# Polysketch attention followed by an RWKV channel mix: four half-batch stages replaced by a batch-wise pipeline with a list-scheduled issue order

## The chip, the cores and the metric

The kernel runs on one core of one Trainium2 chip. The metric is the device time of one execution in microseconds (us). The profile of one execution gives a "span", from its first to its last instruction; the time of the same execution lies about 2 us above it (130.03 and 128.0 us for the changed kernel). PE is the matmul engine, PEld its weight loads, DVE the vector engine, ACT the scalar engine, POOL the GpSimd engine, SP the engine that issues most DMAs.

Each execution is marked fast or slow; slow means over 1.5% above the fastest run of the same kernel. A ratio is the mean time of one kernel's fast runs over the mean of the other's fast runs in the same rounds, so it is not quite the ratio of the medians that stand beside it.

## The reference

The inputs are q, k and v of 4 batches, 4 heads, 1088 tokens and 32 columns, all f32. Each head's q and k are turned into 64 features: `S1` and `S2` (8 x 32 each) give two vectors of 8, and the features are their outer product. The attention is linear, so that a sum over all tokens of a batch is needed before any token of that batch can be finished. The output of the attention then goes through a token shift, two matmuls with a squared ReLU between them, and a sigmoid gate.

```python
def phi(x):
    a = einsum('rd,bhsd->bhsr', S1, x)
    b = einsum('rd,bhsd->bhsr', S2, x)
    return einsum('bhsi,bhsj->bhsij', a, b).reshape(..., 64)
q_p, k_p = phi(q), phi(k)
kv = einsum('bhsf,bhsd->bhfd', k_p, v)          # needs every token of the batch
z = sum(k_p, axis=2)
x = (q_p @ kv) / (q_p . z + 1e-6)               # (4, 1088, 128) after merging heads
# ... the RWKV channel mix
xk = mu_k * x + (1 - mu_k) * x_prev             # x_prev: the token before, 0 at the start
xr = mu_r * x + (1 - mu_r) * x_prev
out = sigmoid(xr @ w_r) * (relu(xk @ w_k)**2 @ w_v)    # w_k 128 x 1024, w_v 1024 x 128
```

## The kernel before

It works on halves (two batches each), with 64 tokens of each of two batches on the 128 partitions. It makes the features of K of half 0, then of half 1 mixed with those of Q of half 0, and only then starts the channel mix ("MoE" below) in one loop over groups of 512 rows. Matmuls for the sums of K look like this; the sum z comes from a matmul of its own:

```python
for h in range(H):
    for b2 in range(2):                       # the two batches of this half
        rows = slice(64 * b2, 64 * b2 + 64)
        nc.tensor.matmul(kv[hp:hp + 64, b2, ...], kp[rows, t - t0, h]..., tok["v%d" % half][rows, h, t, :], ...)
for b2 in range(2):
    nc.tensor.matmul(kv[:64, b2, 64:64 + HR], ab[rows, t - t0]..., ab[rows, t - t0, :, 1, :], ...)
# ... cut: the transposes of K and q, partly on DVE (transp_hd), partly as PE matmuls with the identity (transp_tok)
```

The last stage is a fixed loop that mixes the MoE of one group with the Q features of groups further on:

```python
for n in range(nn + 3):
    g, cp = divmod(n, 4)
    if n < nn: mm1(g, cp)                     # h = w_k^T XK, then relu on ACT
    if cp == 0 and g + 3 < NQ: q1(g + 3)      # features of q, group g+3
    if cp == 1 and g + 2 < NQ: q5(g + 2)      # x = qp . kv, token shift
    # ... cut: q2, Q4, rr, sq
    if 2 <= n < nn + 2: mm2(*divmod(n - 2, 4))   # o += k^2 w_v
    if n >= 6 and cp == 2: fin(g - 1)
```

## Time and profile before

Three runs: 143.38, 139.47 and 143.05 us (median 143.05).

| | kernel before |
|---|---|
| profile span | 136.2 us |
| first MoE matmul (L347) | 64.1 us |
| busy share PE / DVE / ACT | 73% / 57% / 51% |
| share of the longest chain: PE / DVE / ACT / DMA / issue | 50% / 18% / 13% / 8% / 8% |

These are lines of the page of the kernel before: its span, the busy time of each engine (share of the span, and number of records), the clock row (tenths of full rate in 40 slices), the queue that carries instructions (packets, MB, share of 16 DMA engines), and the shares of the chain that ended last.

```profile
span 136.2 us, 4574 instructions
PE 98.8 (73%) x2054; PEld 75.1 (55%) x2065; DVE 78.3 (57%) x155; ACT 69.2 (51%) x117; POOL 8.4 (6%) x29
PEclk9999999986999999999999999986999999999998
q8 instruction: 16, 0.26, 0.8%
PE 50%; DVE 18%; ACT 13%; DMA 8%; issue 8%; SPq 1%; DVEq 0%; ACTq 0%
```

No engine is near full, and the chain goes through all of them. The word "issue" is time in which an engine waited for nothing that the profile shows: 8% of the span.

The same chain in order of time (start in us, length in us, what):

```profile
18.91 1.92 issue
23.33 1.71 PE tp L154 x32
26.04 2.59 issue
37.66 0.87 PE tp L154 x32
64.08 0.39 PE h L347
```

The same 32 K transposes take 1.71 us at 23 us and 0.87 us at 37.7 us, so PE ran at half rate in the first part, although the clock row shows 9 there. The MoE starts at 64 us.

The table by stretches of the kernel before shows which engine works when. Its columns are the stretch, its length, busy us and records of PE, PEld, DVE, ACT and POOL, the granted clock, the DMA share and GB/s.

```profile
0.00:30.00 30.00, 15.59 (x413) 13.55 (x417) 10.19 (x26) 3.56 (x7) 8.45 (x29) 0.99 0.94 244
30.00:60.00 30.00, 25.64 (x928) 21.97 (x924) 13.32 (x24) 11.39 (x28) 0.00 (x0) 0.95 0.02 4
60.00:90.00 30.00, 21.48 (x297) 14.48 (x298) 22.67 (x46) 22.05 (x37) 0.00 (x0) 1.00 0.03 11
```

DVE and ACT, which carry the MoE's squares and ReLUs, do little in the first 60 us. This is the room that the change goes for. The inputs arrive in the first 30 us (DMA share 0.94).

### The profile page before, as it was taken

To read this page: it belongs to the slowest core of one execution; us is meant where nothing else is said; L and a number is where in the kernel's file an instruction comes from. 1 tells how busy PE (TensorE), PEld (TensorE's weight loads), DVE (VectorE), ACT (ScalarE), POOL (GpSimd) and SP (SyncE) were. 2 spreads that over 40 slices of the span, in tenths; PEclk is the share of its full clock that TensorE was granted. 3 is DMA by queue.
4 is the path that set the end of the run, shared out by engine and by line. 5 is a ranking of instruction groups with operands and counts; after the bars stand their busy time and mean duration, and the time that the engine had idled before them with its cause. 6 is when DMAs were issued, how large, how long until landed. Compare 5 with 4: busy or idle time off the path is not lost.

```text
span 136.2 us, 4574 instructions
## 1 busy us (share of the span) xinstructions
PE 98.8 (73%) x2054; PEld 75.1 (55%) x2065; DVE 78.3 (57%) x155; ACT 69.2 (51%) x117; POOL 8.4 (6%) x29
## 2 busy tenths in 40 slices
PE   3250958659997789496929949549949689698970
PEld 2140948458896658374626646346645466465650
DVE  3685030300158572285799595595396795977761
ACT  4010011101461423626886777674687767989950
POOL 7802004000000000000000000000000000000000
PEclk9999999986999999999999999986999999999998
DMA  3999999930000000000000002002002011021013
GB/s 103 335 275 305 301 248 224 302 58 5 5 5 0 5 5 5 7 0 5 0 2 5 0 0 82 0 0 77 0 0 82 0 40 42 0 77 76 5 77 115
DMA packets 5010, 9.79 MB, mean 72 GB/s; under 512 B 1520, under 2 KB 1904, under 8 KB 4992
## 3 DMA queue, kind: packets, MB, share of 16 engines
q1 hardware_dynamic: 3120, 6.69, 16.0%
q0 software_dynamic: 1856, 2.82, 8.9%
q8 instruction: 16, 0.26, 0.8%
q14 instruction: 2, 0.02, 0.0%
q10 hardware_dynamic: 16, 0.00, 0.0%
HBM read 7.80 MB, written 2.23 MB: 74 GB/s over the span
## 4 chain that ended last, share of the span: by engine, by line
PE 50%; DVE 18%; ACT 13%; DMA 8%; issue 8%; SPq 1%; DVEq 0%; ACTq 0%
PE kv L188 9%; DMA tok_v_66<-in_v_dram 8%; PE tp L154 8%; PE qtp L277 7%; PE o L367 7%; PE h L347 6%; DVE qp L270 5%; DVE XK L333 4%; PE abwp L250 4%; PE abp L166 4%; PE kv L195 3%; PE xps L317 2%; ACT PP_150 L332 2%; ACT PP_149 L332 2%; DVE den L262 1%
## 5 line engine op out<-in xcount | busy, mean ns | idle before, releaser
L174 DVE TENSOR_TENSOR kp<-ab 128x1024 f32<-128x1024 f32 (+1 forms) x10 | 10.6, 1064 | 23.3 <-ACT ab L170 23.1
L277 PE MATMUL qtp<-ident,qp 128*128 128x128 f32 x68 | 9.7, 284 | 13.9 <-DVE qp L270 11.8
L347 PE MATMUL h<-XK,wk 128*128 128x512 bf16 (+1 forms) x61 | 18.7, 374 | 0.5
L170 ACT COPY ab<-abp 128x256 f32<-128x256 f32 (+1 forms) x10 | 3.4, 341 | 26.6 <-PE abp L166 26.4
L277 PEld LDWEIGHTS qtp<-ident,qp 128*128 128x128 f32 x68 | 7.4, 142 | 16.9 <-ACT r L381 13.1
L188 PE MATMUL kv<-tok_v_66,kp 64*64 64x32 f32 x272 | 9.6, 269 | 8.1 <-issue 4.5
L188 PEld LDWEIGHTS kv<-tok_v_66,kp 64*64 64x64 f32 x272 | 8.9, 185 | 9.7 <-issue 9.7
L195 PE MATMUL kv<-ab 64*64 64x32 f32 x136 | 11.3, 243 | 0.0
L270 DVE TENSOR_TENSOR qp<-an,abw 128x1024 f32<-128x1024 f32 (+1 forms) x9 | 10.5, 1165 | 0.3
L317 PE MATMUL xps<-qpT,kvbd 128*64 128x256 f32 (+3 forms) x80 | 9.4, 359 | 0.0
L195 PEld LDWEIGHTS kv<-ab 64*64 64x64 f32 x136 | 8.6, 163 | 0.0
L283 ACT COPY qpT<-qtp 128x512 f32<-128x512 f32 (+1 forms) x9 | 5.1, 566 | 4.8 <-PE qtp L277 4.8
L166 PE MATMUL abp<-SW,kT_131 128*32 128x64 f32 x136 | 5.0, 314 | 3.5 <-DVE kT_131 L147 3.5
L285 DVE COPY qpT<-qtp 128x512 f32<-128x512 f32 (+1 forms) x9 | 5.9, 651 | 2.5 <-PE qtp L277 2.5
L188 PE MATMUL kv<-tok_v_67,kp 64*64 64x32 f32 x272 | 6.5, 222 | 0.8 <-issue 0.8
L333 DVE SCALAR_TENSOR_TENSOR XK<-xps,mu_k,PP_150 128x512 bf16<-128x512 f32 (+1 forms) x5 | 3.2, 644 | 6.5 <-ACT PP_150 L332 6.5
L188 PEld LDWEIGHTS kv<-tok_v_67,kp 64*64 64x64 f32 x272 | 5.9, 133 | 1.8 <-issue 1.5
L317 PEld LDWEIGHTS xps<-qpT,kvbd 128*64 128x64 f32 x80 | 4.5, 136 | 4.1 <-issue 1.7
L154 PE MATMUL tp<-ident,tok_k_68 128*32 128x128 f32 x136 | 6.5, 345 | 0.2 <-ACT qpT L283 0.2
L156 ACT COPY kT_132<-tp 128x512 f32<-128x512 f32 (+1 forms) x5 | 2.6, 523 | 7.9 <-PE tp L154 7.9
L347 PEld LDWEIGHTS <-wk 128*128 128x128 bf16 x72 | 5.7, 99 | 0.9 <-issue 0.7
L386 DVE TENSOR_TENSOR osb<-o,r 128x512 f32<-128x512 f32 (+1 forms) x9 | 5.9, 655 | 0.5 <-PE o L367 0.5
(235 smaller groups left out, 215.4 us busy)
## 6 DMA issues: line engine op xcount, KB each, us to landing
out_dram<-osb SPq DMA_DIRECT2D x7, 256.0 KB, 2.0
hd_k_70<-in_k_dram SPq DMA_DIRECT2D x1, 544.0 KB, 4.0
tok_v_66<-in_v_dram POOLq DMA_DIRECT2D x1, 544.0 KB, 8.4
hd_k_71<-in_k_dram SPq DMA_DIRECT2D x1, 544.0 KB, 5.7
tok_v_66<-in_v_dram SPq DMA_DIRECT2D x1, 544.0 KB, 11.5
tok_k_68<-in_k_dram POOLq DMA_DIRECT2D x1, 544.0 KB, 10.4
tok_k_68<-in_k_dram SPq DMA_DIRECT2D x1, 544.0 KB, 15.9
tok_q_69<-in_q_dram POOLq DMA_DIRECT2D x1, 544.0 KB, 12.5
```

Source lines behind the costliest of these rows:

```text
L154: nc.tensor.matmul(tp[D * h:D * h + D, t * P:t * P + P], tok[x][:, h, t0 + t, :], ident[:], skip_group_check=True, tile_position=(0, D * h))
L166: nc.tensor.matmul(abp[32 * c:32 * c + 32, t * 64:t * 64 + 64], kT[half][:, t0 + t, 32 * c:32 * c + 32], SW[:, 0, :, :2, :], skip_group_ch ...
L174: nc.vector.tensor_mul(kp[:, :n], _ap(a_, list(a_.ap[1:]) + [[0, R]]), _ap(b_, list(b_.ap[1:3]) + [[0, R]] + [b_.ap[3]]))
L188: nc.tensor.matmul(kv[hp:hp + 64, b2, (h // 2) * D:(h // 2) * D + D], kp[rows, t - t0, h].rearrange("p i j -> p (i j)"), tok["v%d" % half] ...
L195: nc.tensor.matmul(kv[:64, b2, 64:64 + HR], ab[rows, t - t0].rearrange("p h x r -> p (h x r)"), ab[rows, t - t0, :, 1, :], start=False, st ...
L270: nc.vector.tensor_mul(qp[g][:, :n], _ap(a_, list(a_.ap[1:]) + [[0, R]]), _ap(b_, list(b_.ap[1:3]) + [[0, R]] + [b_.ap[3]]))
L277: nc.tensor.transpose(p[:, t * P:t * P + P], qp[g][:, t, 2 * pair:2 * pair + 2].rearrange("p h i j -> p (h i j)"), ident[:])
L285: nc.vector.tensor_copy(o, p[:, :n * P])
L317: nc.tensor.matmul(o[64 * pair:64 * pair + 64], kvbd[:, 2 * half + b2, pair, :], qpT[g][:].rearrange("p r t (b s) -> p r t b s", b=2)[:, p ...
L333: nc.vector.scalar_tensor_tensor(XK[:, half * NT + T:half * NT + T + m, :].rearrange("p t s -> p (t s)"), src, mu_k[:], PP[half][:, T:T + ...
L347: nc.tensor.matmul(h[:, c, :n * P], wk[:, (2 * cp + c) * P:(2 * cp + c + 1) * P], XK[:, 4 * g:4 * g + n, :].rearrange("p t s -> p (t s)"))
L367: nc.tensor.matmul(ops[g][:, t * P:t * P + P], k2[:, c, t * P:t * P + P], wv[:, 2 * cp + c, :], start=(cp == 0 and c == 0 and t == 0), sto ...
```

## The change

The intent is to start the MoE after one batch instead of after all the features, and to keep every engine supplied from then on.

- The stages run batch by batch. A batch's 1088 tokens lie in 9 slots of 128.
- q is loaded by head and slot and transposed in 32 x 32 blocks on DVE; K is transposed on PE.
- The sums kv and z come from one accumulation: the moving operand is v's 32 columns followed by 32 ones. The K sums are 288 matmuls with 32 columns of weights each.
- Each piece of work becomes a task with an engine, a duration, what it depends on and which buffer it takes. A list scheduler in the build sets the order in which instructions are issued.
- Zero matmuls are put where the plan shows PE idle before 20 us, to keep its clock up (33 in all: 9 at the start, 24 in gaps).
- All PSUM copies of the transposed q features go to ACT; before, half of them were on DVE.

```diff
+NWARM = 9
+KARR = [5.3, 14.2, 21.3, 24.8]           # when the plan expects k of each batch
+T0F, FILL, COLD = 5.3, 20.0, 8.0
+# ... VARR, QARR, WARR, T0, TAU, HOP cut
-                    nc.tensor.matmul(kv[hp:hp + 64, b2, ...], kp[rows, t - t0, h]..., tok["v%d" % half][rows, h, t, :], ...)
-                nc.tensor.matmul(kv[:64, b2, 64:64 + HR], ab[rows, t - t0]..., ab[rows, t - t0, :, 1, :], ...)
+                for x in range(2):
+                    hp = 64 * (h % 2) + 32 * x
+                    nc.tensor.matmul(kv[hp:hp + 32, (h // 2) * 64:(h // 2) * 64 + 64],
+                                     y[:, t, h, 4 * x:4 * x + 4]..., _ap(vh, [[off, 2], [1, D]]), ...)   # v, then ones
+    T["KT" + n] = Task("PE", .35, lambda ...: kt_pe(b, i), [KARR[b]], [("aux", ["KTA" + n])], mode=2)
+    T["AB" + n] = Task("PE", .17, ...)
+    T["KV" + n] = Task("PE", .36, ...)
+    # ... some 380 further tasks cut
+    order, start, end = list_order(T, slots, HOP, WINDOW, SWITCH, COLD)
+    busy = T0F
+    for n in order:
+        if T[n].eng == "PE":
+            if busy < start[n] < FILL:
+                fill(int((start[n] - busy) / (0.43 if busy < COLD else 0.22)))     # zero matmuls
+            busy = end[n]
+        T[n].emit()
```

## The prediction

> **What bounds the kernel now.** No engine does. In the busy table PE has 73% of the span, DVE 57%, ACT 51%; the chain of waits runs through all (PE 50%, DVE 18%, ACT 13%, DMA 8%). Until the first MoE matmul (L347, 64.1 us in the chain in order of time) the features of K and Q are made: DVE works 10.2 us of the first 30 and 13.3 of the next 30, ACT 3.6 and 11.4 (table by stretches). The kv sums wait for v until 13.6 us. From 64 us the MoE takes 9 to 10 us per group of 512 rows, in one serial loop: XK, den, qp on DVE, qtp on PE, o and h matmuls, relu on ACT, PP, XK again. DVE and ACT are then busy about 74%.
>
> The page's clock row shows 9 at the start, but durations contradict it: 32 K transposes (L154) take 1.71 us at 23 to 32 us and 0.87 at 37.7. PE ran at half rate until about 34 us. [...]
>
> **What the change does.** MoE can start after batch 0 alone. With start-to-start times of the trace (ACT: relu of 1024 columns 0.92 us, 512 columns 0.47; DVE: qp of 1024 1.14, square 0.61, XK of 512 0.67) I sum the new kernel:
> - ACT about 70 us: relu 31.5, sigmoid 4, copies of kT, ab, abw, qpT 20, PP and XB 11.5, rest 3. Old sum about 58.
> - DVE about 73 us: kp 10.5, qp 10.5, q transposes 6, den chains 8.5, XK 7.5, squares 21, outputs 5, rest 4. Old sum about 66.
> - PE about 65 us warm; kv and z take 288 matmuls where 680 ran (27.4 us busy before); zero matmuls only fill gaps.
>
> So the change adds elementwise work; it removes waiting, and half-clock PE in the first 34 us.
>
> **Fill.** k of batch 0 lands near 5 us (before, the first k load landed 4.0 us after issue). Chain: kT, ab, three kp (2.6), kv, z, q1, den 1.2, qp, qtp, qpT, xps, PP, XK: about 15 us with hand-overs, so the first MoE matmul is at about 20 us instead of 64. By then ACT and DVE have done 12 to 14 us of work; some 57 us remain on each. If the in-order queues, two shared PSUM buffers and one o buffer let them run at 85%, that takes 67 us; the tail (squares, o matmuls, output product, four DMAs issued in turn) adds 4. Span about 92 us. The times lie 3 to 7 us above the profile's 136.2, so I predict **97 us, range 89 to 108**. Faster by over 2%: 0.97; within 2%: 0.01; slower: 0.02.
>
> **What would show it.** First L512 matmul at 18 to 24 us; 12 K transposes in about 0.35 us from about 8 us on; from 20 us to the tail DVE and ACT at least 80% occupied by start-to-start time; no wait for input DMA over 2 us after the first; no long wait of PE on fin for the single o buffer.
>
> **What would make it wrong.** Arrivals later than the order written into the kernel assumes: the order is fixed, so one late tensor stalls everything behind it, and the counted zero matmuls leave a gap in which the clock drops. [...] The two shared PSUM buffers (about 85 uses, each PE to ACT and back) may hold occupancy to 70%: span 105. Occupancy near 95% would give a span near 84.

Its sum is 20 + 67 + 4, put at about 92 us of span, and 5 us more for the time.

## The result and the profile after

The changed kernel took 130.03, 129.87 and 130.20 us in its fast runs (135.08 in a slow one). The ratio to the kernel before is 0.938, with a 95% interval of 0.927 to 0.950. It is faster, as predicted, but by 6% and not by the predicted 32%: 130 us lies well outside the range of 89 to 108.

The same lines of the page of the changed kernel:

```profile
span 128.0 us, 4696 instructions
PE 103.3 (81%) x2061; PEld 70.5 (55%) x2075; DVE 74.4 (58%) x148; ACT 77.3 (60%) x156; POOL 11.2 (9%) x44
PEclk9999999999769999999999999999999999999996
q8 instruction: 16, 0.26, 0.9%
PE 59%; ACT 13%; DVE 10%; issue 8%; DMA 4%; ACTq 1%; another core or an unknown queue 0%; DVEq 0%
```

DVE and ACT do about what I had summed (74.4 and 77.3 us against 73 and 70). PE is busy 103.3 us, where I had 65. The chain now runs through PE for 59% of the span.

The chain of the changed kernel in order of time, up to the first MoE matmul:

```profile
1.51 5.45 DMA S<-in_S_dram
12.32 1.31 PE ktp L284 x24
16.86 1.17 issue
22.82 2.21 issue
26.25 0.79 PE ktp L284 x24
30.50 3.00 issue
39.83 0.38 PE h L512
```

The MoE starts at 39.8 us, not at 20. Three stops called "issue" take 6.4 us of that (1.17 + 2.21 + 3.00). The first work waits for the small matrix S until 7.0 us. PE is at half rate until about 13 us (24 records of K transposes: 1.31 us at 12.32 us, later 0.79), although the clock row shows 9 there as well.

The list of waits of the changed kernel (engine, what waited, for what: us in total, times, longest) names the instructions that stood at those stops:

```profile
DVE S8r L229 <- DMA S<-in_S_dram: 3.2, 1, 3.2
PE qtp L408 <- issue: 3.0, 1, 3.0
PE abwp L377 <- issue: 2.2, 1, 2.2
PE kv L321 <- issue: 1.2, 1, 1.2
```

They have nothing in common: a transpose, a feature matmul, a sum. What they share is their place in PE's instruction stream. Counted from 0, with weight loads, matmuls and the few waits of PE's sequencer together, the last records before the three stops are 448, 704 and 960, that is 256 apart. In the kernel before, the stops at 18.91 and 26.04 us stand at 448 and 704 too, and two short ones at 42.3 and 46.1 us (0.87 and 0.84 us) at 1728 and 1984, also multiples of 256 further on.

The table by stretches of the changed kernel, with the two stretches after the first MoE matmul cut at the batch periods (a batch is 8 ReLUs of 1024 columns in two groups of 512 rows):

```profile
0.00:20.00 20.00, 15.53 (x311) 10.07 (x311) 6.11 (x18) 4.32 (x11) 11.16 (x44) 1.00 1.00 220
20.00:40.20 20.20, 14.16 (x253) 8.51 (x243) 9.62 (x27) 7.45 (x21) 0.00 (x0) 0.92 0.67 146
40.50:63.90 23.40, 21.19 (x500) 15.37 (x502) 18.38 (x34) 17.97 (x37) 0.00 (x0) 1.00 0.09 21
63.90:86.30 22.40, 21.23 (x500) 15.36 (x502) 15.75 (x27) 18.09 (x37) 0.00 (x0) 1.00 0.09 20
```

In the steady part PE is busy 21.2 of 23.4 and 22.4 us (91% and 95%), ACT 77% and 81%, DVE 79% and 70%. PE's figures are a little too low, since 12 and 13 of a batch's 16 h matmuls have a record here. So the missed 36 us of span (92 expected, 128.0 measured) fall into two parts: 19.8 us before the first MoE matmul (39.8 instead of 20) and 16.2 us after it (88.2 instead of 72).

### The profile page after: what moved, and what is told of

Read it like the earlier page. It is cut to its first block, busy times and chain, and to the rows that moved or that the text cites. A ratio compares the mean times of both kernels' runs of the same rounds, so it can differ in the third digit from the quotient of the medians.

```text
span 128.0 us, 4696 instructions
## 1 busy us (share of the span) xinstructions
PE 103.3 (81%) x2061; PEld 70.5 (55%) x2075; DVE 74.4 (58%) x148; ACT 77.3 (60%) x156; POOL 11.2 (9%) x44
## 3 DMA queue, kind: packets, MB, share of 16 engines
q1 hardware_dynamic: 7762, 6.82, 23.1%
## 4 chain that ended last, share of the span: by engine, by line
PE 59%; ACT 13%; DVE 10%; issue 8%; DMA 4%; ACTq 1%; another core or an unknown queue 0%; DVEq 0%
PE o L531 9%; PE ktp L284 9%; PE h L512 7%; PE qtp L408 7%; PE kv L321 6%; ACT k L517 6%; PE xps L427 5%; PE abwp L377 5%; PE zps L222 5%; DVE XK L442 5%; DMA S<-in_S_dram 4%; PE abp L295 3%; ACT qpT L417 2%; ACT kT L288 2%; DVE k L523 2%
## 5 line engine op out<-in xcount | busy, mean ns | idle before, releaser
L517 ACT ACTIVATE k<-h 128x1024 bf16<-128x1024 f32 (+1 forms) x36 | 35.2, 994 | 4.5 <-PE h L512 2.2
L523 DVE TENSOR_TENSOR k<-k 128x1024 bf16<-128x1024 bf16 (+1 forms) x36 | 23.4, 659 | 11.8 <-ACT k L517 11.7
L531 PE MATMUL o<-wv,k 128*128 128x128 bf16 x272 | 20.9, 220 | 1.4 <-DVE k L523 1.1
L531 PEld LDWEIGHTS <-k 128*128 128x128 bf16 x272 | 16.4, 99 | 7.4 <-DVE k L523 3.4
L417 ACT COPY qpT<-qtp 128x384 f32<-128x384 f32 x24 | 10.7, 498 | 7.8 <-PE qtp L408 7.8
L307 DVE TENSOR_TENSOR kp<-ab 128x768 f32<-128x768 f32 x12 | 11.5, 955 | 4.1 <-ACT ab L300 4.1
L222 PE MATMUL zps<-zero 128*128 128x512 bf16 x33 | 11.7, 476 | 1.0 <-DVE warm L155 1.0
L321 PE MATMUL kv<-tv,kp 128*32 128x64 f32 x576 | 10.7, 221 | 1.2 <-issue 1.2
L284 PE MATMUL ktp<-ident,tk 128*32 128x128 f32 x288 | 11.5, 309 | 0.0
L402 DVE TENSOR_TENSOR qp<-an,abw 128x768 f32<-128x768 f32 x12 | 11.1, 953 | 0.1
## 6 DMA issues: line engine op xcount, KB each, us to landing
tv<-in_v_dram POOLq DMA_DIRECT2D x3, 256.0 KB, 10.8
```

The costliest lines, as they stand in the source:

```text
L222: nc.tensor.matmul(zps[:], zero[:], _ap(zero[:], [[0, 4], [1, P]]), skip_group_check=True)
L284: nc.tensor.matmul(p[D * h:D * h + D, t * P:t * P + P], tk[b][:, h, 3 * i + t, :], ident[:], skip_group_check=True, tile_position=(0, D * h))
L307: nc.vector.tensor_mul(y[:], _ap(a_, list(a_.ap[1:]) + [[0, R]]), _ap(b_, list(b_.ap[1:3]) + [[0, R]] + [b_.ap[3]]))
L321: nc.tensor.matmul(kv[hp:hp + 32, (h // 2) * 64:(h // 2) * 64 + 64], y[:, t, h, 4 * x:4 * x + 4].rearrange("p i j -> p (i j)"), _ap(vh, [[ ...
L417: nc.scalar.copy(x[:], src)
L517: nc.scalar.activation(x[:, :, :w], live.pop(("h", g, cp))[:, :, :w], RELU)
```

## The theories

**T1, fill:** PE stops at block boundaries of its instruction stream, because the fetch of the next block waits while the input loads fill the DMA engines (DMA share 1.00 before 20 us, 0.67 from 20 to 40.2). The trace shows the fetches: queue q8 moves 16 packets of 16,384 bytes. With 256 records between stops, that is 64 bytes per record, by division. In the changed kernel the first three packets start at 15.22, 22.28 and 30.87 us and take 1.32 to 1.37 us each; the three stops end at 18.03, 25.02 and 33.50 us, 1.3 to 1.5 us after a packet is done. The next packet then starts 4.3, 5.9 and 4.3 us after a stop's end, that is after PE has entered a new block (18.03 to 22.28, 25.02 to 30.87, 33.50 to 37.76); the inputs land until about 35 us. From there on this lag is 0.7 us and less (41.74 to 42.32, 46.24 to 46.84, 52.16 to 52.74), and PE does not stop at a boundary again.

**Rival to T1:** the clock and the hand-overs between engines make the fill long, and the stops only take time in which PE would have waited anyway. A third candidate is the late landing of S.

**T2, steady part:** PE is the limit, because its work is about 90 us and not 65. **Rivals to T2:** ACT is the limit; or the two shared PSUM buffers and the fixed order are (the risk that the prediction named); or the order is poor since the planner was given too short durations.

## The experiments

All runs but one gave a right result; `half_of_o` is wrong. Edits are against the changed kernel. The ratios are those on record; their verdict is "faster" for the changed kernel and "unclear" for every other one, so the argument rests on the first h, the stops and the periods more than on the times. "First h" is the start of the first MoE matmul, "periods" are the distances of the ReLUs 0, 8, 16 and 24, all from the profile.

| run | first h, us | periods, us | span, us | fast times, us | ratio to before (95%) |
|---|---|---|---|---|---|
| changed kernel | 39.8 | 23.4, 22.4, 22.1 | 128.0 | 130.03, 129.87, 130.20 | 0.938 (0.927 to 0.950) |
| changed_again | 40.0 | 23.4, 22.4, 22.1 | 128.2 | 130.25, 129.91, 129.29, 129.72 | |
| no_gap_fill | 37.5 | 23.4, 22.4, 23.6 | 127.1 | 129.18, 128.52, 127.35, 128.16 | 0.927 (0.918 to 0.937) |
| no_zero_matmul | 38.4 | 23.4, 22.4, 23.5 | 128.0 (slow) | 127.23, 125.50 | 0.913 (0.896 to 0.931) |
| late_loads | 32.1 | 26.2, 22.4, 23.6 | 124.5 | 126.65, 125.10 | |
| S_first | 41.2 | 23.4, 22.4, 22.1 | 129.4 | 131.41, 130.99, 130.74 | 0.947 (0.940 to 0.955) |
| kv_64_columns | 34.3 | 23.6, 22.6, 22.3 | 123.1 | 125.12, 123.90, 124.68 | |
| half_of_o | 43.4 | 22.6, 21.5, 22.5 | 129.9 (slow) | 128.45, 126.88 | |
| half_qpT_on_DVE | 38.8 | 24.0, 22.9, 24.4 | 130.3 | 132.29, 131.66, 133.33 | |
| twice_h | 39.5 | 25.1, 24.1, 23.4 | 133.3 | 135.37, 135.83, 136.54 | 0.978 (0.968 to 0.989) |
| fewer_wide | 34.8 | 24.1, 23.1, 22.7 | 124.9 | 126.98, 126.39, 125.55, 126.66 | 0.910 (0.902 to 0.918) |
| wide_late_S | 31.5 | 24.1, 23.1, 22.7 | 121.6 | 123.83, 125.57, 124.15 | 0.896 (0.885 to 0.908) |
| measured_durations | 39.4 | 21.7, 23.2, 23.1 | 128.1 | 130.11, 130.55, 131.59, 131.67 | 0.943 (0.933 to 0.952) |
| mixed_tiles_fill | 29.6 | 28.5, 22.6, 22.3 | 123.1 | 125.16, 125.61, 125.61, 125.69 | 0.901 (0.894 to 0.908) |
| mixed_tiles_no_fill | 30.5 | 25.2, 22.6, 22.3 | 120.7 | 122.78, 124.04 | 0.885 (0.862 to 0.908) |
| mixed_tiles_q2 | 29.4 | 24.4, 22.6, 22.3 | 118.9 | 120.89, 122.15 | 0.883 (0.871 to 0.895) |

From the ReLU 24 to the end it is 19.4 to 19.7 us in every run but `twice_h` (20.3). The third period of `no_gap_fill`, `no_zero_matmul`, `late_loads`, `half_qpT_on_DVE` and `half_of_o` is not used below: in each of these runs the clock was at half rate for 3.4 us between 98 and 109 us, after PE had been idle for 1.8 to 2.3 us. The changed kernel has the same idle time of 1.8 us there and kept its clock.

### no_gap_fill and no_zero_matmul: are the zero matmuls worth their place?

```diff
-T0F, FILL, COLD = 5.3, 20.0, 8.0
+T0F, FILL, COLD = 5.3, 0.0, 8.0        # no_gap_fill
-NWARM = 9
+NWARM = 0                              # no_zero_matmul: this as well
```

> The 24 zero matmuls between the stages of the fill are taken out, the 9 at the start stay. Theory A (they hold the clock): without them PE falls back to half rate in the fill; 24 recorded K-transpose matmuls take about 1.3 us instead of 0.79 at 26 us, the first h matmul comes 2 to 5 us later than 39.8 us, time 132 to 135 us. Theory B (real matmuls take longer than the list assumed, so they stand in the way: 5.9 us of the chain of waits is zps): first h matmul 2 to 5 us earlier, time 125 to 128 us.

> All 33 zero matmuls out. Theory A: at half rate until well after 13.6 us, first h matmul at 42 us or later, time over 132 us. Theory B: the 9 at the start run while PE would be idle anyway and so cost nothing; the result is like the run without the gap fill, 125 to 128 us, unless their warm-up matters.

Without the gap fill the first MoE matmul came 2.3 us earlier (37.5), although the stops did not shrink, as the chain of `no_gap_fill` shows:

```profile
14.68 2.03 issue
22.24 3.98 issue
34.28 1.03 issue
37.48 1.02 PE h L512 x4
```

The sum of the three stops is 7.0 us (6.4 in the changed kernel, 6.7 in its repetition), and the clock was at half rate from 19.1 to 29.3 us. That should have cost time, and still the fill was shorter. So 24 zero matmuls, planned for gaps, stood in the way of work: the plan's gaps were not where the real ones are. All zero matmuls together took 10.8 us of PE in the changed kernel, and 5.9 us of the chain. `no_zero_matmul` took 127.23 and 125.50 us in its fast runs, so that the nine at the start are not shown to be needed either; its profile is of a slow run.

### late_loads: are the stops due to input loads?

The loads of k and v of batches 2 and 3 and of q of batch 3 wait until the first batch is nearly through; q of batch 2 is loaded early.

```diff
-    for b in range(2, B):
-        load_tok(tk[b], k, b, 1, nc.gpsimd); load_tok(vv(b), v, b, 1, nc.gpsimd); load_b(b)
+    nc.sync.dma_start(hq[2][:], q[2]...)
+    def late_loads():                     # called after the first PP of batch 0
+        nc.gpsimd.tensor_copy(gate[:, 1:2], PP[0][:1, :1])
+        nc.sync.dma_start(gate[:, 2:3], PP[0][:1, 1:2])
+        # ... the same loads
```

> k, v of batches 2 and 3 and q of batch 3 are held until the PP of batch 0 is done, so that input loads stop near 20 us instead of 31. Theory F (the idle times of PE put down to issue, at its instructions 448, 704 and 960, are instruction fetches that queue behind the input loads): the gap at 448 (1.2 us, at 16.9 us) stays, those at 704 and 960 (2.2 and 3.0 us) shrink to under 0.8 us; the first h matmul comes 3 to 5 us earlier, time about 126 us. Rival: the fetches are slow by themselves or PE waits for something else: the gaps stay within 0.5 us of 2.2 and 3.0.

The stops at 704 and 960 are gone, and the first MoE matmul moved from 39.8 to 32.1 us. Lines of the chain of `late_loads`:

```profile
16.43 0.83 issue
32.09 1.02 PE h L520 x4
38.74 2.55 issue
```

The stop at record 448, while the inputs still load, stays. Where no load is in the way, at record 704, the next packet starts 1.5 us after the boundary (21.80 to 23.29); at record 960, also without loads, it starts as late as 3.3 us after it (27.16 to 30.46), but lands before PE needs it. A new stop of 2.55 us appears at 38.7 us, at record 1472, and this is where the held loads now run (31 to 45 us); the lag before it is 4.5 us (33.97 to 38.48). The stops follow the loads, at whichever block boundary PE then passes; this is what T1 says and the rival does not. The moved stop falls in the first period, which grew by 2.8 us.

### S_first: is it the late S?

```diff
+    nc.sync.dma_start(S8[:, 0, :], S1)
+    nc.scalar.dma_start(S8[:, 1, :], S2)
     load_tok(tk[0], k, 0, 0, nc.sync)
     load_tok(tk[0], k, 0, 1, nc.scalar)
-    nc.sync.dma_start(S8[:, 0, :], S1)
-    nc.scalar.dma_start(S8[:, 1, :], S2)
```

> The two 1 KB loads of S1 and S2 are issued before the K loads. They landed at 7.0 us, behind 544 KB of k, and PE stood until 7.3 us although k was there at 6.5. Expected: sps at about 3 to 4 us, the first K transpose at about 6.9 us instead of 9.0, everything after about 2 us earlier, time about 128 us. If instruction fetch paces the fill instead, the gaps take the gain back: first h matmul within 0.7 us of 39.8, time within 0.7 us of 130.

The K transposes began at 7.2 us instead of 9.0, and yet the first MoE matmul came at 41.2 us, 1.4 us later. Two of the stops in the chain of `S_first`:

```profile
21.73 3.58 issue
32.24 2.64 issue
```

With the stop at 448 (1.9 us) they add to some 8.1 us. PE reached the first two block boundaries 2.2 and 1.1 us earlier, but the packets of the next two blocks did not come earlier (22.54 and 31.86 us, against 22.28 and 30.87). So the gain seems lost in the stops, as the second half of my expectation had it, but the first MoE matmul lies outside the 0.7 us that it allowed. Two more things differ here, and no run separates them: q of batch 1 landed at 20.0 us instead of 15.4, and DVE stood 0.6 us for it ahead of work that PE needed; and the clock fell to half rate twice before the MoE (at 25.1 and 35.4 us) instead of once.

### kv_64_columns and fewer_wide: the same loads, fewer instructions

`kv_64_columns` uses one matmul with 64 columns of weights for two of 32. `fewer_wide` does that as well, uses one matmul of 128 columns for four of 32 in the K and Q features, and 64 columns in x.

```diff
-                for x in range(2):
-                    hp = 64 * (h % 2) + 32 * x
-                    nc.tensor.matmul(kv[hp:hp + 32, ...], y[:, t, h, 4 * x:4 * x + 4]..., ...)
+                hp = 64 * (h % 2)
+                nc.tensor.matmul(kv[hp:hp + 64, ...], y[:, t, h]..., ...)
# fewer_wide, besides:
-            for c in range(4):
-                o = (3 * i + t) * P + 32 * c
-                nc.tensor.matmul(p[32 * c:32 * c + 32, t * 64:t * 64 + 64], kT[b % 2][:, o:o + 32], SW..., ...)
+            o = (3 * i + t) * P
+            nc.tensor.matmul(p[:, t * 64:t * 64 + 64], kT[b % 2][:, o:o + P], SW..., ...)
# and likewise in q1_pe and x_pe
```

> kv sums with 64-column stationary tiles: half as many matmuls (24 recorded per group instead of 48), the same result. If the small matmuls are paced per instruction (17 ns each recorded one), a group falls from 0.81 to about 0.41 us, PE gets 4.8 us less work, instruction blocks are used up more slowly in the fill, and the time falls by 3 to 6 us. If they are paced by loading columns (the number of columns stays), a group stays at 0.75 to 0.9 us and the time moves less than 1.5 us, but for the fetch gaps.

> ab and q1 with 128-column stationary tiles (one matmul per 128 tokens instead of four), kv and xps with 64: the same results with about 770 fewer matmuls and as many fewer weight loads. Theory F (the fill is paced by instruction fetches behind the input loads): fewer blocks of 256 are used up before the first h matmul, at most one gap over 1 us remains, first h matmul at 30 to 34 us instead of 40, time 121 to 124 us. From kv with 64 columns (same time per group as with 32) the work of PE per batch should hardly change: period 21.5 to 22.5 us.

With 288 fewer matmul records in all and 72 fewer per batch (and as many fewer weight loads), `kv_64_columns` kept one stop (2.7 us, at 704) and gained 5.6 us before the first MoE matmul. `fewer_wide` records 1296 matmuls instead of 2061, has no stop above 0.1 us before its first MoE matmul, and starts the MoE at 34.8 us under the same loads; from its chain:

```profile
34.77 0.38 PE h L507
```

So T1 holds from the other side too: with fewer block boundaries in the loading time, fewer stops.

The steady part did not gain. These are the groups of the kv sums in one batch period, in the changed kernel and then in `kv_64_columns` (line, engine, operation, names, shapes, number of records, then busy us and mean ns, then idle time before them):

```profile
L321 PE MATMUL kv<-tv,kp 128*32 128x64 f32 x144 | 2.6, 221 | 0.0
```

```profile
L320 PE MATMUL kv<-tv,kp 128*64 128x64 f32 x72 | 2.8, 226 | 0.0
```

Half the instructions take about the same time, so a matmul with 32 columns of weights costs about half as much as one with 64 (2.6 us for 72 issued, 36 ns each; 2.8 us for 36, 78 ns each). As many columns took about the same time; in the changed kernel 48 loads of 32 columns passed in 0.81 us (a kv task), 1.9 columns per ns. That loading the columns is what sets the time, as the expectation words it, is not shown. The wide features even cost more: the periods of `fewer_wide` are 0.6 to 0.7 us longer, where I had expected no change. In these kernels narrow tiles are good for the steady part and bad for the fill (first MoE matmul at 39.8 us against 34.8).

### twice_h and half_of_o: is PE the limit of the steady part?

`twice_h` runs each group's even h matmul twice, to the same place. `half_of_o` leaves out half of the o matmuls; its result is wrong (relative error 0.73).

```diff
# twice_h
-            nc.tensor.matmul(h[:, c, :w], wk[...], XKf[...])
+            for _ in range(2 - c):
+                nc.tensor.matmul(h[:, c, :w], wk[...], XKf[...])
# half_of_o, in mm2
-        for c in range(2):
+        for c in range(1, 2):
```

> Half of the h matmuls (one of each pair of chunks) are issued twice: 36 more matmuls, 7.3 us of PE at 216 ns, nothing for ACT, DVE or loads, same result; 1.73 us per batch of 8 steps. Theory P (PE is the limit from 40 to 105 us): the batch period rises from 22.4 to about 24 us and the time by 5 to 7 us. Rival R (hand-overs in the fixed order): idle time takes most of it up, the time rises by less than 3 us. A mixture, as the run with half of the o matmuls gave (1.0 us less per batch for 1.8 us taken away): 3 to 5 us.

> Wrong result on purpose: of each pair of chunks only one is multiplied with w_v, which takes 136 of the 272 o matmuls (about 7.6 us at 56 ns) from PE and nothing from ACT, DVE or the loads. Theory P (from 40 to 105 us PE is the limit): the 16 chunks steps per batch get 3.6 us shorter, the batch period falls from 23 to about 20 us, time 123 to 125 us. Rival R (hand-overs between PE, ACT and DVE in the fixed order, with two shared PSUM buffers, are the limit): the time falls by less than 2.5 us.

The table by stretches of `twice_h`, for its first two batch periods:

```profile
40.40:65.50 25.10, 22.98 (x507) 16.12 (x510) 18.17 (x34) 18.32 (x37) 0.00 (x0) 1.00 0.09 20
65.50:89.70 24.20, 23.13 (x508) 16.25 (x511) 15.76 (x27) 18.48 (x37) 0.00 (x0) 1.00 0.08 17
```

PE's busy time rose from 21.19 and 21.23 to 22.98 and 23.13 us, and these two periods by 1.7 us each (the third by 1.3). Added PE work, about 1.7 us a batch, goes into these periods one for one, with DVE and ACT unchanged. PE holds 84% of the chain in the two periods; the rest passes through DVE, ACT and short stops.

The same stretches of `half_of_o`:

```profile
44.10:66.60 22.50, 20.01 (x471) 13.55 (x470) 18.04 (x34) 17.72 (x36) 0.00 (x0) 1.00 0.11 23
66.60:88.10 21.50, 20.19 (x472) 13.54 (x470) 15.72 (x27) 17.95 (x37) 0.00 (x0) 1.00 0.09 20
```

It removes 1.8 us of PE per batch (8 steps of 4 matmuls of 56 ns; the larger figure in my expectation was a slip, a batch has 8 steps). The periods fell by 0.85 and 0.93 us, about half of it. PE's busy time above falls by only 1.2 and 1.0 us, partly because more h matmuls have a record here (16 and 17 against 12 and 13). The profile is of a slow run, but the clock was full in both stretches; the fast times, 126.9 and 128.5 us, are some 2 us below `changed_again`, which is within what I had left to the rival. So PE is the limit, as `twice_h` shows, but perhaps with little room below it: after about 0.9 us something else may hold, and I did not settle what.

### half_qpT_on_DVE: is ACT the limit?

```diff
-  lambda b=b, i=i, p=pair, o=on_act: qtp_ev(b, i, p, o)
+  lambda b=b, i=i, p=pair: qtp_ev(b, i, p, p == 0)      # the second pair's copy on DVE; order of issue unchanged
```

> Same order of issue, but the second qpT copy of each pair is done by DVE instead of ACT: ACT loses 12 copies (5 us), DVE gains 12 (about 5.8 us). Theory P: PE is the limit, both others have slack, the time stays within 1.5 us of 130. If ACT were the limit as predicted (70 us of work), the time falls by 3 us or more; if DVE is close to the limit, it rises by 3 us or more.

It takes 12 of the 24 copies (about 0.5 us each) from ACT. The periods rose by 0.5 us in the two that can be compared, and the fast times to between 131.7 and 133.3 us. So ACT is not the limit. That the copies now come later in DVE's fixed order would explain the rise; no run separates this.

### measured_durations: was the order poor because the plan had wrong durations?

```diff
-KT .35, AB .17, KV .36, WP .2, Q1 .26, XP .36
+KT .80, AB .54, KV .81, WP .37, Q1 .60, XP .68      # as the trace shows them
```

> Only the durations given to the list are changed, to those measured for the small f32 groups (K transpose 0.80 instead of 0.35, ab 0.54 for 0.17, kv 0.81 for 0.36, q1 0.60 for 0.26, xps 0.68 for 0.36, w 0.37 for 0.20), so that order and zero matmuls follow what PE really does. If the order is what costs time in the steady part, the batch period falls by 0.7 us or more and the time by 2 to 4 us; if PE's work does, the period stays within 0.5 us of 22.4, and the time moves by the fill alone (fewer zero matmuls: up to 2 us less).

The first period fell by 1.7 us and the next two rose by 0.8 and 1.0; the fast times are 130.1 to 131.7 us. Right durations in the same list scheduler moved the work about and gained nothing. This rival falls, for this scheduler.

### wide_late_S and the mixed tiles: is there a better kernel?

`wide_late_S` joins fewer_wide, late_loads, S_first and no gap fill.

> The run with fewer, wider matmuls, and also the later loads for batches 2 and 3, S first and no zero matmuls in gaps (the 9 at the start stay). No gap of fetch over 0.7 us before the first h matmul, which comes at 25 to 28 us; the clock may fall to half in the fill without the gap fill, which would cost 1 to 2 us there. Time 115 to 119 us.

Its fast runs took 123.8 to 125.6 us, where I had expected 115 to 119. Its first MoE matmul came at 31.5 us, held up by a new wait: DVE stood 2.9 us for q of batch 1, whose transposes came ahead of other work in DVE's fixed order.

The mixed kernels use wide tiles only in the fill and narrow ones in the steady part, load S first, and tell the plan that q of batch 1 comes at 18 us. `mixed_tiles_no_fill` also leaves the gap fill out. `mixed_tiles_q2` keeps the gap fill and moves the load of q of batch 2 ahead.

```diff
-QARR = [8.6, 12.4, 23.9, 27.5]
+QARR = [8.6, 18.0, 23.9, 27.5]
+            if b == 0 or (b == 1 and i == 0):     # abp and kv wide; q1 wide only for b == 0
+                ...                               # as in fewer_wide
+            else:
+                ...                               # as in the changed kernel; x always 64 columns
# mixed_tiles_q2, besides: ahead of the gate that holds back batches 2 and 3
+    nc.sync.dma_start(hq[2][:], q[2].rearrange("h (a s) d -> (h a) s d", s=NS))
```

> Wide tiles (few instructions) only for batch 0 and the first third of batch 1, the narrow ones of the changed kernel after that, xps with 64 columns throughout; S first; the q transposes of batch 1 placed after 18 us, so that DVE does not stand before a late load; the zero matmuls in gaps kept. If instruction fetch is what paced the fill and column loading what paces the steady part: no fetch gap over 0.7 us before the first h matmul, which comes at 32 to 33.5 us with the clock full throughout, and the batch period is back at 22 to 22.5 us (23.1 to 24.1 with wide tiles everywhere): time 121 to 124 us. If the period stays at 23 us or above, the wide tiles were not what lengthened it.

> The same without the zero matmuls in gaps. With the fetches out of the way the remaining question of the fill is whether the zero matmuls pay: if they only stand in the way, the first h matmul comes 3 to 5 us earlier (28 to 30 us), time 117 to 120 us; if the clock falls without them, 24 recorded K-transpose matmuls in the fill take 1.3 us instead of 0.8 and the gain is under 2 us.

> As mixed_tiles_fill, with the load of q of batch 2 moved ahead of k and v of batch 2 on its queue. In that run DVE stood 4.6 us at 30 to 34.8 us before the first q transpose of batch 2, waiting for this load, and the first batch period was 28.5 us instead of 22.5. If that wait is what made it long, the period falls to 22.5 to 24 us and the time to 119.5 to 122 us; if only the wait moves on (to k or v of batch 1 or 2, or to w_k), the time stays above 123 us.

In `mixed_tiles_fill` the MoE starts at 29.6 us. Its first period is 28.5 us, for a reason that its list of waits (28 to 45 us) gives:

```profile
DVE qT L382 <- DMA hq<-in_q_dram: 4.6, 1, 4.6
```

Now that the work is early, q of batch 2 is late. With that load moved ahead (`mixed_tiles_q2`), the first period fell to 24.4 us, and the kernel took 120.89 and 122.15 us, the best, 0.883 of the kernel before. Its page:

```profile
span 118.9 us, 4155 instructions
PE 101.2 (85%) x1791; PEld 70.1 (59%) x1805; DVE 73.8 (62%) x148; ACT 77.3 (65%) x156; POOL 11.8 (10%) x44
```

Its chain up to the MoE has no "issue" above 0.1 us; a few of its lines:

```profile
7.04 1.52 PE ktp L286 x48
10.98 0.65 PE zps L224 x3
17.95 1.50 PE abwp L391 x12
29.39 0.38 PE h L530
```

The K transposes start at 7.04 us and run at full rate from the start (48 records in 1.52 us, against 2.72 in the changed kernel). Between them and the MoE matmul lie 22.4 us, of which zero matmuls take about 4.3 us by the chain. `mixed_tiles_no_fill`, without them, starts the MoE at 30.5 us, with the clock at half rate from 18.9 to 25.8 us. Once the stops are gone, the gap fill is worth about 0.9 us of first MoE matmul (29.6 against 30.5); with the stops it cost 2.3 us. In time the run without it was still the faster of the two (122.8 and 124.0 us against 125.2 to 125.7), since its wait for q of batch 2 was 2.9 us instead of 4.6. Whether the gap fill pays with that load moved ahead was not run.

### changed_again: does the changed kernel repeat?

> The changed kernel unaltered, as the control on the chip of the next three runs. 129 to 131 us where it is not disturbed, with the gaps of PE at its instructions 448, 704 and 960 again, and PE occupied (start to next start) for about 91% of 40 to 105 us, ACT 78%, DVE 73%.

Its edit is none. In another job it took 129.29 to 130.25 us, with the same periods to 0.01 us. It stopped at the same three records, for 0.9, 3.9 and 2.0 us instead of 1.2, 2.2 and 3.0: the places repeat, the lengths do not.

## Why the prediction was wrong

**Right.** Faster, and by the named route: the MoE starts earlier, and DVE and ACT have the work that I summed (73 and 70 us predicted, 74 and 77 measured). That no engine bounded the kernel before is in line with its profile. No wait of PE, DVE or ACT for an input was above 2 us but the first, that for S of 3.2 us; the stops are not waits for data. PE did not wait long for the single o buffer.

**"The first MoE matmul is at about 20 us instead of 64."** It was at 39.8 us, so this term of the sum was 19.8 us too small. What the runs showed in its place (the points overlap in time, so they are not a sum):

1. Stops for instruction fetches, 6.4 us on the chain. late_loads and fewer_wide show that they go with the loads and with the number of instructions, and they move the first MoE matmul by 7.7 and 5.1 us.
2. S lands behind k, at 7.0 us; PE's first real work starts at 7.3 us, not at 5. This is about 2 us; S_first, with the stops still there, did not gain it.
3. "Zero matmuls only fill gaps" was false: they take 5.9 us of the chain, and taking the gap fill away starts the MoE 2.3 us earlier.
4. PE at half rate until about 13 us, and again from 33.8 to 37.2 us after the 3.0 us stop. The clock fell after the stop of 3.00 us and not after that of 2.21 us; but it also fell after stops of 2.6 and 2.7 us (S_first, kv_64_columns), was kept through one of 2.55 us (late_loads), and fell in mixed_tiles_no_fill (half rate from 18.9 to 25.8 us) with no single PE gap above about 1.0 us in the 10 us before. So the length of one gap did not decide it here.
5. Matmuls in f32 take about twice what I gave them (next point): "12 K transposes in about 0.35 us" took 0.79 us at full rate.

In the best kernel, where 1 is gone, the MoE starts at 29.4 us. Its 9.4 us over the predicted 20 are 2 us of later start, some 4.3 us of zero matmuls, and a rest of about 3 us, which I put down to point 5 (an estimate, not tested alone).

**"PE about 65 us warm."** This is the step that failed in the second part: measured, PE is occupied for 103.3 us, 10.8 of them zero matmuls, so about 92 us of work. I had taken the time per record for the time per matmul. The prediction shows it where it sets "288 matmuls" against "680": the first number counts matmuls in the program, the second records in the trace. In records it is 576 against 680. In the changed kernel's trace these f32 matmuls leave two records each: the K sums (288 issued, 576 records), the K transposes, which are matmuls with the identity (144, 288), and the x matmuls (48, 96). The transposes of the q features, issued in transpose mode (72, 72), and the bf16 o matmuls (272, 272) leave one. So in the kernel before, the program issues 16 K transposes where the trace has the 32 of the lines above. From the kernel before's own time per record at full rate (K features 20 ns, K sums 20 to 22, o 65, h about 250, transposed q features 126) and the doubled counts one gets an estimate of about 90 us, so all that was needed was in the profile. The f32 matmuls are long in the trace itself: an x task of four matmuls with 384 f32 columns each takes 0.65 us together, and an h matmul of 512 bf16 columns about 0.22 us (two in 0.43 to 0.45 us on the chain of the kernel before). Why is not shown. The constants in the kernel's planner have the same error (0.35 for 0.79, 0.36 for 0.81), and I had read them as support.

**"If the in-order queues ... let them run at 85%, that takes 67 us."** DVE and ACT were occupied, start to start, for 72% and 78% of the time between ReLU 0 and ReLU 24, since PE, occupied for about 90% of it, was the limit: twice_h shows added PE work going into the time one for one. The three periods and the tail took 88.2 us with the last hand-overs, instead of 72. The sum of the two parts, 19.8 + 16.2 = 36.0 us, is the whole gap from 92 to 128.0.

**The risks named.** "A gap in which the clock drops" came true (half rate from 33.8 to 37.2 us, after the 3.00 us stop), though not from a late tensor. "The two shared PSUM buffers" as the cause of 70% occupancy is not shown; PE's own work is enough to explain the periods, and what holds 0.9 us below it is open. I had also counted 3 to 7 us from span to time, by setting the times of some runs against the span of another; for this kernel it was 2.0.

**Left open.** Why a fetch starts 4 to 6 us late during loads is not shown directly; one of the late starts (37.76 us) lies some 3 us after the last input landed. The lags with loads (4.3 to 5.9 us) and without (0.7 us and less) fit T1, but the 3.3 us without loads in late_loads do not, and no run varied the packets. What limits the steady part just below PE is open as well.

## What to carry to other kernels

Before costing a change, divide an engine's busy time by the instructions the program issues, not by the records in the trace, and compare the total with every engine's, not only with the busiest ones of before. While the inputs load, count PE's instructions: in these kernels each 256 could cost a stop of 0.8 (late_loads) to 4.0 us (no_gap_fill), so use few wide matmuls there and narrow ones later, and hold back loads that are not needed yet. In a kernel with a fixed order, look for the next late tensor after each gain, and keep zero matmuls only where a run shows that they are not in the way.
